# Who makes the low parts of w1's and w2's words: from GpSimd and three VectorE passes to VectorE and, for half of them, a second ScalarE pass

## The chip, the core and the metric

The kernel runs on one core of a Trainium2 chip (trn2). A core has five engines that run side by side, each taking its own instructions strictly in the order in which the program put them: TensorE (PE in the profile; the load of its weights is PEld), VectorE (DVE), ScalarE (ACT), GpSimd (POOL) and SyncE (SP, which here only issues DMAs). SBUF is the on-chip memory of 128 partitions, PSUM the accumulator that TensorE writes. The metric is the device time of one execution in microseconds (us); lower is better.

## The reference

Three layers stand one behind the other. Causal attention with a decay bias over 4 batches, 8 heads, 576 positions and a head size of 64; then a gated product through four weights; then a soft mixture of 8 experts. What matters here is the second layer:

```python
def _moe_ref(x, w1, w2, w3, w_out):      # x 2304x512, w1 and w2 512x1024
    a = x @ w1
    b = x @ w2
    h = a * b @ w3
    return (h @ w_out).astype(np.float32)
```

The four weights reach the chip as 64-bit floats, seen as pairs of 32-bit words, and the kernel makes 32-bit floats of them itself.

## The kernel before

The attention comes first, per item (a head and some of its five query tiles): `att_scores` multiplies on PE into a PSUM tile `sc_ps` (L359), takes bias, mask and row maximum on DVE (L362) and the exponent on ACT (L367). `att_norm` sums and inverts on DVE (L376, L377) and scales the tile `sc` by the inverse on POOL (L380). `att_transpose` turns `sc` on PE (`pt_ps` L395, `ptd_ps` L409) and copies it on ACT (L397, L411), and `att_pv` multiplies by the values on PE (`x_ps`, L110) and splits the result into a high and a low part on ACT and DVE (L444, L445).

The gated product `glu_half` (L457, `gl`) multiplies a split x by a split weight: high by high, low by high and high by low, for four blocks of 128 rows, so twelve matmuls for one PSUM tile. Its weights are the tiles `w12t_0` to `w12t_7`, each with a high and a low part, and each made of two halves of 128x512 words. So w1 and w2 are 16 halves, k = 0 to 15, and `load_words(k)` handles one of them:

- SP fetches 512 KB into `raw_w` (L188; three such buffers, NRAW = 3, so the fetch of half k + 3 waits until half k's words have been read).
- `convert` makes the float `w`. With `by_act` false: one ACT pass scales the upper word (L202), and three DVE passes shift (L205), put in the sign (L206) and put in the lower word's bits (L209). With `by_act` true: a second ACT pass turns the lower word in place (L213), and two DVE passes join the three (L214, L217). Before the change w1 and w2 take the first form; the 24 halves of `wot` and `w3t` that follow take the second.
- ACT rounds `w` to the high part (L233), and POOL subtracts to get the low part (L234).

The order in which the Python code calls these steps is woven from lists (`weave`): the halves 0 to 7 among the attention's first part, 8 to 15 further on among the first gated products. The order on PE, DVE, ACT and POOL is then set by a scheduler that reckons its own times, so an edit in one place reorders the queues around it and behind it; SP's order is the written one. The scores use four PSUM tiles in turn, the values and the transposes two each.

Of the kernel before, what the change touches and what calls it, by code (L numbers as in the profile page):

```python
# [10 lines left out]
F32 = mybir.dt.float32  # L11
# [5 lines left out]
ALU = mybir.AluOpType  # L17
# [30 lines left out]
def attn_glu_softmoe_kernel(  # L48
# [14 lines left out]
    nc = tc.nc  # L63
# [127 lines left out]
    def convert(k, w, by_act, behind=None):  # L191
        raw = words.pop(k)
        pair = raw.bitcast(I32).rearrange("p (n t) -> p n t", t=2)
        hi, lo = pair[:, :, 1], pair[:, :, 0]
        wi, wu = w.bitcast(I32), w.bitcast(U32)
        order = mybir.DependencyInfo(mybir.DependencyClass.NoSync, mybir.DependencyReason.DATA)

        def line_up(step):
            if behind is not None:
                tc.add_manual_dep(step.ins, behind.ins.name, order, reason="order")  # L200

        line_up(nc.scalar.activation(out=w, in_=hi.bitcast(F32), func=AF.Copy, scale=F64_SCALE))  # L202
        lu = lo.bitcast(U32)
        if not by_act:
            nc.vector.tensor_scalar(out=wi, in0=wi, scalar1=3, scalar2=None, op0=ALU.logical_shift_left)  # L205
            nc.vector.scalar_tensor_tensor(  # L206
                out=wi, in0=hi, scalar=-0x80000000, in1=wi, op0=ALU.bitwise_and, op1=ALU.bitwise_or
            )
            return nc.vector.scalar_tensor_tensor(  # L209
                out=wu, in0=lu, scalar=29, in1=wu, op0=ALU.logical_shift_right, op1=ALU.bitwise_or  # L210
            )

        line_up(nc.scalar.activation(out=lo, in_=lu, func=AF.Copy, scale=LO_SCALE, bias=-0.49999))  # L213
        nc.vector.scalar_tensor_tensor(  # L214
            out=wi, in0=wi, scalar=3, in1=lo, op0=ALU.logical_shift_left, op1=ALU.bitwise_or
        )
        return nc.vector.scalar_tensor_tensor(  # L217
            out=wi, in0=hi, scalar=-0x80000000, in1=wi, op0=ALU.bitwise_and, op1=ALU.bitwise_or
        )
# [4 lines left out]
    def load_words(k, ap):  # L224
        (kind, i), e = TODO[k // 2], k % 2
        span = slice(512 * e, 512 * e + 512)
        if kind == "w12":
            if e == 0:
                w12_t[i] = wp.tile([P, 2, 2, KC, P], F32R, tag="W", name=f"w12t_{i}", bufs=NW)
            w = gq.tile([P, 512], F32, tag="g4", name=f"w_{kind}_{i}_{e}", bufs=NG4)  # L230
            convert(k, w, False)
            th, tl = (w12_t[i][:, n].rearrange("p a k f -> p (a k f)")[:, span] for n in range(2))
            nc.scalar.copy(out=th, in_=w)  # L233
            nc.gpsimd.tensor_tensor(out=tl, in0=w, in1=th.bitcast(F32), op=ALU.subtract)  # L234
        elif k < 2 * N0:
            if e == 0:
                rows_t[kind, i] = gq.tile([P, FC, P], F32, tag="g4", name=f"{kind}_{i}", bufs=NG4)
            rows_w[kind, i] = convert(k, rows_t[kind, i].rearrange("p c f -> p (c f)")[:, span], True)
        else:
            if e == 0:  # L240
                rows_t[kind, i] = ap.tile([P, 1024], F32, tag="words", name=f"w_{kind}_{i}", bufs=NRAW)
            convert(k, rows_t[kind, i][:, span], True, st["a_copy"])
# [514 lines left out]
    with tc.tile_pool(name="att", bufs=1) as ap:  # L757
# [11 lines left out]
            out=mask[:, S - P :], in_=mask[:, S - P :], pattern=[[-1, P]], base=0,  # L769
# [27 lines left out]
        def load(k):  # L797
            i = k // 2 - 1
            if FC <= i < N0:
                (sum_rows if k % 2 else use_rows)(*TODO[i])  # L800
            if k < 2 * N0:
                load_words(k, ap)
            if k + NRAW < 2 * N0:
                fetch_words(k + NRAW, ap)
# [10 lines left out]
        for i in range(N0, len(TODO)):  # L815
            more += [(1, lambda i=i: fetch_later(i)), (1, lambda: None)]
            more += [(1, lambda k=2 * i + e: load_words(k, ap)) for e in range(2)] + [(1, lambda: None)]
# [8 lines left out]
        k = GC - GB  # L826
# [75 lines left out]
    for a in range(0, 4, 2):  # L902
        zt_ps = psum("tp", f"zt_ps_{a}")
        for c in range(2):
            nc.tensor.transpose(zt_ps[:, c * P : (c + 1) * P], z_acc[:, (a + c) * P : (a + c + 1) * P], ident)
        nc.vector.tensor_reduce(
            out=zt[:, a : a + 2], in_=zt_ps[:, : 2 * P].rearrange("p (c t s) -> p c s t", t=2, s=2 * NS),
# [233 lines left out]
```

## Time and profile before

| what | value |
| --- | --- |
| median of 3 runs | 550.09 us (549.1 to 554.26) |
| the profiled execution | 552.43 us, of which the span from first to last instruction is 550.7 us |
| PE busy | 516.8 us, 94% of the span |
| DVE busy | 329.0 us, 60% |
| ACT busy | 311.6 us, 57% |
| POOL busy | 130.6 us, 24% |

A busy PE is not yet a PE at its peak, since the ends of its matmuls are modelled. Shares of busy time are means over stages that have different limits, so the rows further down are taken by stage: to 46 us the attention stands nearly alone, from 46 to 83 us attention, the words of w1 and w2 and the first gated products run together, to 175 us the words of `wot` and `w3t` join, and from there to 490 us gated products, attention and the experts' gates fill PE.

### The profile page before, as it was taken

To read this page: it belongs to the slowest core of one execution; us is meant where nothing else is said; L and a number is where in the kernel's file an instruction comes from. 1 tells how busy PE (TensorE), PEld (TensorE's weight loads), DVE (VectorE), ACT (ScalarE), POOL (GpSimd) and SP (SyncE) were. 2 spreads that over 40 slices of the span, in tenths; PEclk is the share of its full clock that TensorE was granted. 3 is DMA by queue.
4 is the path that set the end of the run, shared out by engine and by line. 5 is a ranking of instruction groups with operands and counts; after the bars stand their busy time and mean duration, and the time that the engine had idled before them with its cause. 6 is when DMAs were issued, how large, how long until landed. Compare 5 with 4: busy or idle time off the path is not lost.

```text
span 550.7 us, 11764 instructions
## 1 busy us (share of the span) xinstructions
PE 516.8 (94%) x4288; PEld 434.3 (79%) x4288; DVE 329.0 (60%) x1016; ACT 311.6 (57%) x845; POOL 130.6 (24%) x199
## 2 busy tenths in 40 slices
PE   2799899998999999999999999999999999989993
PEld 2567678877788898999989889899989999843452
DVE  7558787879987394866577668566630311252433
ACT  4567667687986674866577567558644211321222
POOL 4475563102454232110221311111310000000000
PEclk9999989999999999999999999999999999999998
DMA  5746973977673253563656537553514999689977
GB/s 147 235 146 193 280 223 128 292 259 269 218 253 102 73 161 113 169 201 133 194 170 211 173 99 208 176 172 114 167 44 137 413 411 376 241 293 423 420 295 241
DMA packets 38809, 118.03 MB, mean 214 GB/s; under 512 B 4224, under 2 KB 10560, under 8 KB 35296
## 3 DMA queue, kind: packets, MB, share of 16 engines
q1 hardware_dynamic: 36768, 113.60, 61.0%
q10 hardware_dynamic: 1984, 3.69, 2.4%
q8 instruction: 34, 0.56, 0.4%
q14 instruction: 23, 0.19, 0.1%
HBM read 102.11 MB, written 11.60 MB: 206 GB/s over the span
## 4 chain that ended last, share of the span: by engine, by line
PE 70%; DMA 13%; DVE 8%; ACT 4%; issue 2%; POOL 1%; SPq 0%; ACTq 0%; DVEq 0%; POOLq 0%
PE gl L457 31%; PE sc_ps L359 7%; PE x_ps L110 7%; PE pt_ps L395 5%; DMA raw_w<-in_w 5%; PE gn_ps L627 3%; PE o_ps L1042 3%; DMA raw_w3t<-in_w3t 3%; PE h_ps L1004 3%; PE ptd_ps L409 2%; PE z_ps L110 2%; DMA raw_wot<-in_wot 2%; DVE sc L362 1%; PE lg L110 1%; ACT sc L367 1%
## 5 line engine op out<-in xcount | busy, mean ns | idle before, releaser
L457 PE MATMUL gl<-x,w12t 128*128 128x320 f32 (+1 forms) x1536 | 237.7, 304 | 0.1
L457 PEld LDWEIGHTS gl<-x,w12t 128*128 128x128 f32 x1536 | 212.7, 190 | 7.4 <-issue 4.4
L380 POOL TENSOR_SCALAR sc<-sc,rinv 128x64 f32<-128x64 f32 (+4 forms) x160 | 101.1, 650 | 253.0 <-DVE rinv L377 85.7
L367 ACT ACTIVATE sc<-sc,nmax 128x64 f32<-128x64 f32 (+4 forms) x160 | 89.8, 563 | 31.4 <-DVE nmax L362 29.1
L362 DVE CUSTOM_DVE_ANT_0 sc<-sc_ps,mask 128x64 f32<-128x64 f32 (+4 forms) x160 | 65.0, 423 | 31.8 <-PE sc_ps L359 31.0
L397 ACT COPY pt<-pt_ps 128x128 f32<-128x128 f32 (+3 forms) x128 | 53.0, 426 | 34.1 <-PE pt_ps L395 25.1
L395 PE MATMUL pt_ps<-ident,sc 128*128 128x128 f32 x320 | 56.6, 286 | 5.5 <-POOL sc L380 3.2
L395 PEld LDWEIGHTS pt_ps<-ident,sc 128*128 128x128 f32 x320 | 38.4, 144 | 16.9 <-POOL sc L380 7.2
L463 ACT COPY a<-gl 128x256 f32<-128x256 f32 (+1 forms) x64 | 25.4, 398 | 46.0 <-PE gl L457 40.7
L359 PE MATMUL sc_ps<-qa 128*128 128x64 f32 (+1 forms) x144 | 46.4, 334 | 1.3 <-DVE gT L475 0.8
L110 PE MATMUL x_ps<-pt,v 128*64 128x256 f32 (+1 forms) x384 | 47.4, 358 | 0.0
L359 PE MATMUL sc_ps<-raw 68*128 68x288 f32 (+4 forms) x96 | 35.8, 516 | 11.6 <-DMA raw<-rows 9.8
L359 PE MATMUL sc_ps<-qb 68*128 68x64 f32 (+1 forms) x144 | 43.6, 306 | 0.9 <-DMA qb<-qa 0.9
L110 PEld LDWEIGHTS x_ps<-pt,v 128*64 128x64 f32 x384 | 33.5, 140 | 5.8 <-issue 1.0
L359 PEld LDWEIGHTS sc_ps<-raw 68*128 68x128 f32 x96 | 21.6, 265 | 16.9 <-issue 14.1
L202 ACT ACTIVATE w_w<-raw_w 128x512 f32<-128x512 f32 x32 | 21.6, 676 | 17.8 <-DMA raw_w<-in_w 17.7
L445 DVE TENSOR_TENSOR x<-x_ps,x 128x320 fp32r<-128x320 f32 (+1 forms) x32 | 14.1, 452 | 29.2 <-ACT x L444 29.2
L630 ACT COPY gn<-gn_ps 128x512 f32<-128x512 f32 x40 | 22.5, 584 | 15.5 <-PE gn_ps L627 15.1
L367 ACT ACTIVATION_READ_ACCUMULATOR sc<-sc,nmax 128x1 f32 x160 | 30.9, 193 | 0.0
L359 PEld LDWEIGHTS sc_ps<-qa 128*128 128x128 f32 x144 | 27.4, 190 | 3.6 <-DVE gT L475 1.3
L409 PE MATMUL ptd_ps<-ident,sc 128*128 128x128 f32 x160 | 25.9, 286 | 3.2 <-ACT pt L397 3.0
L359 PEld LDWEIGHTS sc_ps<-qb 68*128 68x128 f32 x144 | 27.4, 191 | 1.6 <-DVE v_sb L276 1.0
(180 smaller groups left out, 725.6 us busy)
## 6 DMA issues: line engine op xcount, KB each, us to landing
ew<-in_ew SPq DMA_DIRECT2D x27, 1024.0 KB
raw_w<-in_w SPq DMA_DIRECT2D x32, 512.0 KB
raw<-in_qk SPq DMA_DIRECT2D x24, 576.0 KB
v<-in_v SPq DMA_DIRECT2D x16, 576.0 KB
raw_w3t<-in_w3t SPq DMA_DIRECT2D x16, 512.0 KB
raw_wot<-in_wot SPq DMA_DIRECT2D x8, 512.0 KB
raw_wo<-in_wo SPq DMA_DIRECT2D x8, 512.0 KB
w_d<-w_w SPq DMA_DIRECT2D x8, 512.0 KB
```

What stands on the lines that cost most here:

```text
L110: mm = nc.tensor.matmul(out_, lhs, rhs, start=start, stop=stop)
L202: line_up(nc.scalar.activation(out=w, in_=hi.bitcast(F32), func=AF.Copy, scale=F64_SCALE))
L359: nc.tensor.matmul(pp[:r, : z - a], x[:, 0, q0 : q0 + r], x[:, 1, a:z], start=x is mul[0], stop=x is mul[-1])
L362: nc.vector.tensor_tensor_reduce(out=sc[:r, a:z], in0=pp[:r, : z - a], in1=hd["mask"][:r, m0 : m0 + z - a], scale=-0.125, scalar=3.0e38 if ...
L367: nc.scalar.activation(out=sc[:r, :W], in_=sc[:r, :W], func=AF.Exp, bias=nmax[:r, i : i + 1], scale=-1.0, accum_out=rsum[:r, i, 0:1],)
L380: nc.gpsimd.tensor_scalar(out=sc, in0=sc, scalar1=rinv[:, i : i + 1], scalar2=1.0, op0=ALU.mult, op1=ALU.mult)
L395: nc.tensor.transpose(tp[:, j * P : (j + 1) * P], sc[:, j * P : (j + 1) * P], ident)
L397: t["turned", i] = nc.scalar.copy(out=pt[:, p0 : p0 + step * (i - 1) + 1 : step], in_=tp[:, : i * P].rearrange("p (j q) -> p j q", q=P))
L409: nc.tensor.transpose(dg[:, p0 : p0 + P], t["sc"][:, c0 : c0 + P], ident)
L457: nc.tensor.matmul(acc[:, :nt], w12_t[fc][:, wi, n, kc], x_t[b, blk, kc][:, xi], start=k == 0, stop=k == 3 * KC - 1)
L463: st["a_copy"] = nc.scalar.copy(out=a_sb[:, :nt], in_=acc[:, :nt])
L630: st["turned", blk, k, h] = nc.scalar.copy(out=gn[:r, 4 * h : 4 * h + 4].rearrange("p c f -> p (c f)"), in_=tp[:r])
```

## The change

Two things change in `load_words`. The low part's subtraction goes from POOL to DVE, for all 16 halves. And `convert` is called with `k >= 8` in the place of `False`, so the last eight halves are converted in the second form: two ACT passes and two DVE passes in the place of one and three.

```diff
@@ load_words
             w = gq.tile([P, 512], F32, tag="g4", name=f"w_{kind}_{i}_{e}", bufs=NG4)
-            convert(k, w, False)
+            convert(k, w, k >= 8)
             th, tl = (w12_t[i][:, n].rearrange("p a k f -> p (a k f)")[:, span] for n in range(2))
             nc.scalar.copy(out=th, in_=w)
-            nc.gpsimd.tensor_tensor(out=tl, in0=w, in1=th.bitcast(F32), op=ALU.subtract)
+            nc.vector.tensor_tensor(out=tl, in0=w, in1=th.bitcast(F32), op=ALU.subtract)
```

SP's queue is the same before and after. On the other engines instructions move. The next rows are POOL's, from the stretch around 46 to 83 us (`w_w_4_0` is half 8: tile 4, half 0; `rinv` comes from L377):

```order
 L380 TENSOR_SCALAR sc_632<-sc_632,rinv_725 128x576
-L234 TENSOR_TENSOR w12t_664<-w_w_4_0_665,w12t_664 128x512
-L234 TENSOR_TENSOR w12t_664<-w_w_4_1_716,w12t_664 128x512
-L234 TENSOR_TENSOR w12t_761<-w_w_5_0_762,w12t_761 128x512
 L380 TENSOR_SCALAR sc_696<-sc_696,rinv_807 128x448
 L380 TENSOR_SCALAR sc_696<-sc_696,rinv_807 128x576
-L234 TENSOR_TENSOR w12t_761<-w_w_5_1_819,w12t_761 128x512
-L234 TENSOR_TENSOR w12t_879<-w_w_6_0_880,w12t_879 128x512
-L234 TENSOR_TENSOR w12t_879<-w_w_6_1_932,w12t_879 128x512
 L380 TENSOR_SCALAR sc_802<-sc_802,rinv_895 128x448
 L380 TENSOR_SCALAR sc_802<-sc_802,rinv_895 128x576
```

Only the attention's scalings stay on POOL, in their old order. On PE, at about 77 us of the trace of before, this piece changes (`sc_802` is the tile that POOL's last two rows above scale):

```order
 L359 MATMUL sc_ps_4_1_903<-raw_585 128x288
-L409 MATMUL ptd_ps_860<-ident,sc_696 128x128 x2
-L395 MATMUL pt_ps_3_912<-ident,sc_802 128x128 x3
 L457 MATMUL gl_0_2_1_917<-x_0_0_111,w12t_433 128x320 x3
 L457 MATMUL gl_0_2_1_917<-x_0_1_157,w12t_433 128x320 x3
 L457 MATMUL gl_0_2_1_917<-x_0_2_181,w12t_433 128x320 x3
 L457 MATMUL gl_0_2_1_917<-x_0_3_253,w12t_433 128x320 x3
+L409 MATMUL ptd_ps_860<-ident,sc_696 128x128 x2
+L395 MATMUL pt_ps_3_912<-ident,sc_802 128x128 x3
```

The transposes of `sc_802` now stand behind twelve gated products, which stood behind them. On DVE, where half 8 and half 9 are converted, before:

```order
L205 TENSOR_SCALAR w_w_4_1_716<-w_w_4_1_716 128x512
L206 SCALAR_TENSOR_TENSOR w_w_4_1_716<-raw_w_4_1_560,w_w_4_1_716 128x512
L209 SCALAR_TENSOR_TENSOR w_w_4_1_716<-raw_w_4_1_560,w_w_4_1_716 128x512
L362 ISA sc_696,nmax_695<-sc_ps_3_0_697,mask 128x448
```

and the same place on DVE now:

```order
L214 SCALAR_TENSOR_TENSOR w_w_4_1_716<-w_w_4_1_716,raw_w_4_1_560 128x512
L234 TENSOR_TENSOR w12t_664<-w_w_4_0_665,w12t_664 128x512
L217 SCALAR_TENSOR_TENSOR w_w_4_1_716<-raw_w_4_1_560,w_w_4_1_716 128x512
L362 ISA sc_696,nmax_695<-sc_ps_3_0_697,mask 128x448
L362 ISA nmax_695 128x1
L362 ISA sc_696,nmax_695<-sc_ps_4_0_730,mask 128x288
L362 ISA nmax_695 128x1
L234 TENSOR_TENSOR w12t_664<-w_w_4_1_716,w12t_664 128x512
```

Each subtraction stands a few instructions behind the last pass on its words: that of half 8 between the two passes on half 9, that of half 9 between two pieces of the attention's maximum (L362). It reads what ACT's L233 wrote, so DVE now waits there for ACT, as POOL did.

## Rows read from the trace of the kernel before

**Rows 1.** Windows by stage: PE, PEld, DVE, ACT, POOL busy (count), PEclk, DMA, GB/s
```profile
7.00:46.00 39.00, 31.97 (x120) 24.10 (x121) 23.76 (x94) 24.16 (x79) 19.27 (x30) 1.00 0.58 168
46.00:83.00 37.00, 33.02 (x216) 26.41 (x215) 31.43 (x72) 25.85 (x64) 22.58 (x18) 0.95 0.83 244
...
175.00:490.00 315.00, 313.59 (x2645) 284.91 (x2643) 170.14 (x553) 176.01 (x487) 51.08 (x92) 1.00 0.57 192
```
**Rows 2.** Waits of PE, 46 to 83 us: total, times, longest
```profile
PE pt_ps L395 <- ACT pt L397: 1.9, 2, 0.9
PE pt_ps L395 <- POOL sc L380: 1.2, 1, 1.2
PE sc_ps L359 <- DVE w_w L205: 0.6, 1, 0.6
```
**Rows 3.** Timeline of PE: start, us, line, tile, [idle before <- releaser]
```profile
78.66 0.68 PE L395 MATMUL pt_ps<-ident,sc 128*128 128x128 f32 x3 [1.19 <-POOL sc L380]
78.99 3.52 PE L457 MATMUL gl<-x,w12t 128*128 128x320 f32 x12
...
86.28 2.14 PE L457 MATMUL gl<-x,w12t 128*128 128x320 f32 x12
```
**Rows 4.** Timeline of POOL around 77 us
```profile
75.83 1.46 POOL L234 TENSOR_TENSOR w12t<-w_w,w12t 128x512 fp32r<-128x512 f32 x1 [1.28 <-ACT w12t L233]
77.27 2.48 POOL L380 TENSOR_SCALAR sc<-sc,rinv 128x448 f32<-128x448 f32 x2
```
**Rows 5.** Windows of 1 us: granted clock of PE is the third number from the end
```profile
78.00:79.00 1.00, 0.34 (x4) 0.35 (x4) 1.00 (x3) 0.82 (x2) 1.00 (x2) 0.97 0.35 115
79.00:80.00 1.00, 1.00 (x6) 1.00 (x5) 0.97 (x2) 0.00 (x0) 1.00 (x2) 0.50 0.90 254
82.00:83.00 1.00, 1.00 (x6) 0.73 (x4) 0.15 (x1) 1.00 (x4) 0.68 (x1) 0.83 0.83 250
```
**Rows 6.** Groups of POOL, ACT and DVE, 46 to 83 us: busy, mean ns, idle before
```profile
L234 POOL TENSOR_TENSOR w12t<-w_w,w12t 128x512 fp32r<-128x512 f32 x10 | 14.7, 1480 | 12.8 <-ACT w12t L233 12.8
L380 POOL TENSOR_SCALAR sc<-sc,rinv 128x448 f32<-128x448 f32 (+1 forms) x8 | 8.0, 1009 | 2.8 <-DVE rinv L377 2.6
...
L233 ACT CAST w12t<-w_w 128x512 fp32r<-128x512 f32 x10 | 6.2, 623 | 3.4 <-DVE w_w L209 3.4
L397 ACT COPY pt<-pt_ps 128x384 f32<-128x384 f32 (+3 forms) x13 | 5.5, 428 | 1.5 <-PE pt_ps L395 1.5
L202 ACT ACTIVATE w_w<-raw_w 128x512 f32<-128x512 f32 x8 | 5.4, 679 | 5.5 <-DMA raw_w<-in_w 5.4
...
L209 DVE SCALAR_TENSOR_TENSOR w_w<-raw_w,w_w 128x512 uint32<-128x512 uint32 x10 | 12.5, 1252 | 0.2
L206 DVE SCALAR_TENSOR_TENSOR w_w<-raw_w,w_w 128x512 int32<-128x512 int32 x9 | 6.9, 768 | 0.1
L205 DVE TENSOR_SCALAR w_w<-w_w 128x512 int32<-128x512 int32 x9 | 3.8, 422 | 3.5 <-ACT w_w L202 3.4
```
**Rows 7.** Single lines, whole span: count, ns min/median/max, first and last start
```profile
L209 DVE SCALAR_TENSOR_TENSOR w_w<-raw_w,w_w x16: 673/1043/1646, 9.3 to 79.2; 128x512 uint32<-128x512 uint32 x16
L214 DVE SCALAR_TENSOR_TENSOR w_w<-w_w,raw_w x16: 682/693/1093, 285.3 to 408.3; 128x512 int32<-128x512 int32 x16
L217 DVE SCALAR_TENSOR_TENSOR w_w<-raw_w,w_w x16: 678/682/823, 287.1 to 409.2; 128x512 int32<-128x512 int32 x16
L213 ACT ACTIVATE raw_w<-raw_w x16: 660/668/717, 284.6 to 407.6; 128x512 int32<-128x512 uint32 x16
```
**Rows 8.** Timeline of DVE and of POOL at 48 us
```profile
48.57 1.65 DVE L209 SCALAR_TENSOR_TENSOR w_w<-raw_w,w_w 128x512 uint32<-128x512 uint32 x1
...
48.00 1.66 POOL L234 TENSOR_TENSOR w12t<-w_w,w12t 128x512 fp32r<-128x512 f32 x1 [3.46 <-ACT w12t L233]
```
**Rows 9.** PE's transposes (L395), to 46 us and from 46 to 77 us: ns min/median/max
```profile
L395 PE MATMUL pt_ps<-ident,sc x15: 421/421/476, 15.3 to 44.2; 128*128 128x128 f32 x15
...
L395 PE MATMUL pt_ps<-ident,sc x30: 271/273/329, 46.6 to 73.4; 128*128 128x128 f32 x30
```
## The prediction

> **What bounds the kernel now.** I read the windows by stage first. From 175 to 490 us PE is busy for 313.59 of 315 us [rows 1]: whatever comes early, PE works it off without a gap, so time won or lost ahead of 175 us arrives at the end nearly whole. The edit's own instructions all lie ahead of 83 us (L209 starts for the last time at 79.2 us [rows 7]). So the question is what PE loses there. Between 46 and 83 us it is busy for 33.02 of 37 us, DVE for 31.43, ACT for 25.85, POOL for 22.58 [rows 1]: PE lacks 3.98 us, DVE is next to full.
>
> Second, I read PE's waits in that window. The long ones are 1.9 us for ACT's copies of transposed tiles, 1.2 us for POOL's scaling (L380) and 0.6 us for DVE [rows 2]. The place of the 1.2 us is at 78.66 us: PE waits 1.19 us for `sc_802` [rows 3]. POOL began that scaling at 77.27 us, the moment at which it finished a subtraction (L234) that had started at 75.83 us [rows 4]. So here the instruction that the edit takes away stands right in front of the one that PE needs.
>
> Third, the granted clock. The gap is followed by a fall: 0.97 in the microsecond in which PE was busy for only 0.34, then 0.50 from 79 us, and 0.83 in the microsecond from 82 [rows 5]. 0.50 is the 1.2 GHz level, 1.00 the 2.4 GHz one. The twelve gated products at 78.99 us took 3.52 us, the same twelve at 86.28 us took 2.14 us [rows 3].
>
> **The change part by part.**
>
> *The wait on POOL.* Without L234, POOL is free when L377 gives the inverse, at most 1.2 us earlier for PE; and the order of after puts twelve gated products (2.14 us at full clock) ahead of the transposes of `sc_802`, more than the gap. I take all of it: -1.2 us. Bounds 0 (another releaser steps in) and -1.2.
>
> *The clock.* If that gap goes, the half-speed stretch goes: full cycles lost are 0.03 + 3 x 0.50 + 0.17 = 1.7 us by the windows 78 to 83 (I show the first, one of three and the last) [rows 5]. The gated products alone give 3.52 - 2.14 = 1.4. I take -1.7; bounds 0 and -1.7.
>
> *DVE, last eight halves.* In 46 to 83 us ten L209, nine L206 and nine L205 took 12.5 + 6.9 + 3.8 = 23.2 us [rows 6]. In their place stand two halves in the old form with a subtraction, and eight in the new one. The subtraction on DVE at this size is in no row. Nearest is L214, two inputs from SBUF at 128x512, 0.693 us; L209's 0.673 and 1.646 are the ends for two inputs at this size [rows 7]. I take 0.69. A new half is 0.693 + 0.682 + 0.69 = 2.07 us; an old one 0.42 + 0.69 + 0.69 + 0.69 = 2.49 without slowing. Together 8 x 2.07 + 2 x 2.49 = 21.5, less 1.1 for the L205 and L206 that fall ahead of 46 us: 20.4. DVE gets back 2.8 us, if the slowing goes away. At 1.646 a piece the ten subtractions cost 9.6 us more, and DVE loses 6.8.
>
> *Why the slowing should go.* L209 takes 0.673 us at its fastest and 1.25 in the mean of this stage [rows 6, 7]. At 48.57 us it took 1.65 us beside a POOL subtraction of 48.00 to 49.66 us, which was itself slowed to 1.66 us; 49.66 + 0.56 is L209's end at 50.22 [rows 8], so one ran behind the other. With the subtraction on DVE that partner is gone. The scalings remain, 8.0 us of POOL in the window [rows 6].
>
> What DVE's 2.8 us are worth to PE: PE waited for DVE directly for only 0.6 us here [rows 2], so between 0 and -1.5 us (that 0.6 and 0.9 of ACT's copies behind it). I take -0.5.
>
> *DVE, first eight halves.* Their passes stay, and each gets a subtraction. Six of the eight lie ahead of 46 us (ten of L209's sixteen lie behind it [rows 6, 7]): 6 x 0.69 = +4.1 us on a DVE that is busy for 23.76 of 39 us [rows 1]. PE, busy for 31.97, is the slower one there, so DVE's 15.2 idle us hide it: 0. Without that cover, up to +4.1.
>
> *ACT.* Eight more passes of 0.668 us [rows 7] make 5.3 us. ACT is idle for 11.15 us from 46 to 83 us, of which 5.4 us it waits for words to land and 3.4 us for L209 [rows 1, 6]. A pass fits into these idles as a sum, but it stands in front of copies that PE waits for: queued behind L202 and L213 are L397 and L411, and PE already waits for L397 for 1.9 us [rows 2]. I take one pass in front of one such copy: +0.6 us. Bounds 0 and +1.9 (both waits grow by one pass and a half).
>
> *DMA.* SP's queue is unchanged. A `raw_w` buffer is freed by L217 in the place of L209, the same number of steps behind its landing (L202, L213, L214, L217 for L202, L205, L206, L209), so refetches start when they did: 0.
>
> Sum: -1.2 - 1.7 - 0.5 + 0.6 = -2.8 us against the profiled execution's 552.43 us, so 549.6. That run lies 0.4% above the median of 550.09; scaled, 547.3 us.
>
> **The rivals.**
>
> *The clock rises earlier (faster).* The same transposes take 421 ns up to 44.2 us and 273 ns from 46.6 us [rows 9]. So PE runs slowly through the first stage, although the granted clock reads 1.00 there, and I go by durations. PE is busy for 31.97 of 39 us in it [rows 1]. If the new order on PE lets the clock rise a quarter of the stage earlier, some 34 us in the place of 44, ten busy microseconds shrink to 10 x 273 / 421 = 6.5: -3.5 us. With the sum's -2.8 and DVE's full -1.5 in the place of -0.5 that is -7.3, so 543. Against it: transfers of the next heads' rows pace that stage too.
>
> *DVE takes over POOL's wait (slower).* POOL sat idle for 12.8 us from 46 to 83 us until ACT's L233 came [rows 6], and that cost only POOL. Now DVE waits there, with L362 behind it, which frees the scores' PSUM for PE. If each of the eight late subtractions holds DVE for two of ACT's copies that stand ahead of L233 and for L233, 2 x 0.428 + 0.623 = 1.48 us [rows 6], that is 11.8 us; less the 2.8 us saved and DVE's 5.6 us of idle time [rows 1], 3.4 us reach PE, and a gap of this kind brings one more fall of the clock beside the old one: 3.4 + 1.2 + 1.7 = +6.3, so 556.5 us. It decides from (2.8 + 5.6) / 8 = 1.05 us a half. Against it: each subtraction stands behind passes on the next half, by which time L233 is mostly done, and DVE already waited 3.4 us for ACT there.
>
> *The scalings take the subtraction's place (no change).* A half of the new form has three passes with two SBUF inputs, the old one has two. Rows 8 show such a pass and a POOL instruction one behind the other. If each of the eight scalings in the window, 8.0 us in all [rows 6], holds DVE for its whole length, DVE loses 8.0 - 2.8 = 5.2 us, all but 0.4 of its idle time. L377 then comes late by about the time that POOL is free sooner, PE waits at the same place for the same scaling, and the clock falls as before: 0, so 550. Against it: the scalings fill 8.0 of 37 us, so most passes meet none. The Trainium skill's page "SBUF — State Buffer", section "Who interferes with whom", states what this rival rests on: a VectorE instruction with two SBUF inputs and a GpSimd instruction that reads SBUF exclude each other for the whole instruction. By that rule, rows 8 agree, and the edit trades one partner of the exclusion for more meetings with the other.
>
> **How the numbers follow.** The forecast, 547.3 us with its own range of 545 to 549.5 us, has 0.45; the early clock 0.30 (543, within 538 to 544.5); DVE's wait 0.15 (556.5, from 555.7 on); the scalings 0.10. One per cent, 5.5 us, is about what a measurement of this kernel can tell from no change. So faster by more than 1% has 0.30, within 1% 0.55, slower 0.15. The range, 540 to 554 us, leaves out the slower case and the far end of the early clock, some 0.2.
>
> **What would show it.** Right: no granted clock below 1.00 between 46 and 83 us, no PE wait for L380 over 0.5 us there, L214 and L217 near 0.69 us, PE idle in that window near 1.5 us less than 3.98. DVE's rival shows as idle time ahead of L234 put down to L233 beyond 1 us a half and as PE waits for L362. The early clock shows in transposes of 273 ns well before 44 us. Wrong it would be if the windows after 175 us were no longer full, or if a gap over 1 us with a fall of the clock came back elsewhere ahead of 100 us.

## The result and the profile after

The changed kernel takes 556.84 us (median of 12 runs, 553.19 to 561.16) against 551.38 us before (12 runs, 548.22 to 554.26) on the same chip: ratio 1.0101, interval 1.0077 to 1.0126. It is slower by 1%, where 547.3 us was forecast and 554 was the upper end. The profiled execution of after is its fastest one (553.19 us, span 551.4 us), that of before lies above its median, so their spans differ by only 0.7 us, and no row of the two profiles can stand for the difference of the medians.

The windows by stage, in the columns of [rows 1], from the trace of after:

```profile
7.00:46.00 39.00, 32.06 (x107) 22.36 (x109) 27.26 (x103) 24.06 (x78) 12.82 (x24) 1.00 0.58 162
46.00:83.00 37.00, 34.03 (x219) 26.24 (x216) 24.90 (x62) 27.58 (x67) 7.75 (x9) 0.91 0.74 217
...
175.00:490.00 315.00, 313.08 (x2652) 284.24 (x2648) 170.25 (x554) 177.42 (x492) 54.07 (x95) 1.00 0.57 191
```

What the edit was to do, it did. From 46 to 83 us DVE is busy for 24.90 us in the place of 31.43, POOL for 7.75 in the place of 22.58, and PE lacks 2.97 us in the place of 3.98. The groups of the same window, beside [rows 6], show how (busy, mean ns, idle before):

```profile
L380 POOL TENSOR_SCALAR sc<-sc,rinv 128x448 f32<-128x448 f32 (+2 forms) x9 | 8.2, 924 | 27.3 <-DVE rinv L377 16.1 <-ACT raw_w L213 8.4 <-ACT x L444 2.7
...
L217 DVE SCALAR_TENSOR_TENSOR w_w<-raw_w,w_w 128x512 int32<-128x512 int32 x8 | 5.8, 724 | 0.0
...
L214 DVE SCALAR_TENSOR_TENSOR w_w<-w_w,raw_w 128x512 int32<-128x512 int32 x8 | 5.5, 692 | 4.7 <-ACT raw_w L213 4.7
L234 DVE TENSOR_TENSOR w12t<-w_w,w12t 128x512 fp32r<-128x512 f32 x8 | 5.5, 686 | 0.4 <-ACT w12t L233 0.2
...
L213 ACT ACTIVATE raw_w<-raw_w 128x512 int32<-128x512 uint32 x8 | 5.3, 668 | 0.0
L233 ACT CAST w12t<-w_w 128x512 fp32r<-128x512 f32 x8 | 5.0, 629 | 1.4 <-DVE w_w L209 1.4
```

The subtraction costs 0.686 us on DVE, 0.69 had been taken; L209, 1.25 us in the mean of [rows 6], is at 0.69 again (one instruction in this window; all eight of after took 676 to 727 ns). The wait of 1.2 us for POOL [rows 2, 3] is gone, and the clock no longer falls behind it [rows 5]. PE's two long waits in the window are new (total, times, longest):

```profile
PE ptd_ps L409 <- ACT pt L397: 1.6, 1, 1.6
PE gl L457 <- ACT x L444: 1.0, 1, 1.0
```

The mean granted clock of the window is 0.91, lower than the 0.95 before. The windows of 1 us say where; the granted clock is the third number from the end:

```profile
47.00:48.00 1.00, 0.70 (x4) 0.29 (x2) 1.00 (x4) 0.27 (x1) 0.03 (x1) 1.00 0.00 0
48.00:49.00 1.00, 0.00 (x0) 0.00 (x0) 0.75 (x3) 1.00 (x3) 0.00 (x0) 1.00 0.70 184
...
51.00:52.00 1.00, 1.00 (x4) 0.59 (x3) 0.00 (x0) 0.57 (x2) 0.14 (x1) 0.62 0.95 361
52.00:53.00 1.00, 1.00 (x3) 0.49 (x2) 0.39 (x1) 0.00 (x0) 0.00 (x0) 0.50 0.91 240
...
57.00:58.00 1.00, 1.00 (x13) 0.81 (x10) 0.00 (x0) 0.00 (x0) 0.90 (x2) 0.50 0.00 0
58.00:59.00 1.00, 1.00 (x13) 0.75 (x11) 0.17 (x1) 0.90 (x4) 0.46 (x1) 0.97 0.00 0
```

PE is idle for most of 47.7 to 49.3 us, the clock falls at 51 us, and PE works at the 1.2 GHz level until 58 us. Full cycles lost: 0.38 + 6 x 0.50 + 0.03 = 3.4 us, twice what the fall at 79 us had cost. The durations show something more, which the granted clock doesn't: in after the transposes of L395 still take 421 to 476 ns at 47.0 to 47.3 us, and those of L409 take 272 to 334 ns from 49.3 us; in before both take 270 to 274 ns from 46.3 us. So PE also reaches the 2.4 GHz level for the first time some 3 us later, and in after it holds it only until 51 us. PE's timeline there, first of before, then of after (start, us, line, tile, [idle before <- releaser]):

```profile
44.37 2.10 PE L359 MATMUL sc_ps<-raw 68*128 68x448 f32 x6
...
47.52 1.96 PE L359 MATMUL sc_ps<-raw 68*128 68x448 f32 x6 [0.61 <-DVE w_w L205]
...
49.78 1.12 PE L457 MATMUL gl<-x,w12t 128*128 128x320 f32 x6
```

```profile
40.99 3.75 PE L359 MATMUL sc_ps<-raw 68*128 68x448 f32 x6
...
49.32 0.55 PE L409 MATMUL ptd_ps<-ident,sc 128*128 128x128 f32 x3 [1.63 <-ACT pt L397]
...
51.05 3.44 PE L359 MATMUL sc_ps<-raw 68*128 68x448 f32 x6
53.88 2.21 PE L457 MATMUL gl<-x,w12t 128*128 128x320 f32 x6
```

These are the same instructions (the profile counts each of the score instructions twice, so x6 stands for three): the scores of item 8 (2.10 before, 3.75 after), the scores of item 9 (1.96, 3.44), the first six gated products (1.12, 2.21), and the gap ahead of them (0.61, 1.63). Together after loses 1.65 + 1.48 + 1.09 + 1.02 = 5.2 us on four rows. That the medians differ by 5.5 us proves nothing by itself, since the two profiled spans differ by 0.7 us: this execution of before paid its 1.2 and 1.7 us at 78 us, and after didn't. The rows show where to look. What differs is the order: after makes the scores of item 8 ahead of the transposes of item 4 and of the values product of items 2 and 3, before made them behind that product, between item 4's transposes. The experiments ask whether it is this order, and which part of the edit brought it.

### The profile page after: what moved, and what is told of

Same layout as the page of the kernel before. It is cut to its first block, busy times and chain, and to the rows that moved or that the text cites. A ratio compares the mean times of both kernels' runs of the same rounds, so it can differ in the third digit from the quotient of the medians.

```text
span 551.4 us, 11754 instructions
## 1 busy us (share of the span) xinstructions
PE 518.7 (94%) x4288; PEld 433.5 (79%) x4288; DVE 328.4 (60%) x1024; ACT 316.3 (57%) x853; POOL 112.5 (20%) x183
## 4 chain that ended last, share of the span: by engine, by line
PE 69%; DMA 12%; DVE 7%; ACT 6%; issue 2%; POOL 1%; SPq 1%; ACTq 0%; DVEq 0%; POOLq 0%
PE gl L457 31%; PE x_ps L110 7%; PE sc_ps L359 6%; DMA raw_w<-in_w 6%; PE pt_ps L395 5%; PE gn_ps L627 3%; PE o_ps L1042 3%; DMA raw_wot<-in_wot 3%; PE h_ps L1004 3%; PE ptd_ps L409 2%; PE z_ps L110 2%; DMA raw_w3t<-in_w3t 2%; DVE sc L362 1%; POOL sc L380 1%; PE lg L110 1%
## 5 line engine op out<-in xcount | busy, mean ns | idle before, releaser
L380 POOL TENSOR_SCALAR sc<-sc,rinv 128x64 f32<-128x64 f32 (+4 forms) x160 | 105.3, 677 | 291.0 <-DVE rinv L377 175.3
L362 DVE CUSTOM_DVE_ANT_0 sc<-sc_ps,mask 128x64 f32<-128x64 f32 (+4 forms) x160 | 65.1, 423 | 35.3 <-PE sc_ps L359 32.3
L395 PE MATMUL pt_ps<-ident,sc 128*128 128x128 f32 x320 | 56.0, 287 | 4.5 <-POOL sc L380 3.2
L395 PEld LDWEIGHTS pt_ps<-ident,sc 128*128 128x128 f32 x320 | 37.9, 145 | 16.2 <-issue 8.0
L359 PE MATMUL sc_ps<-raw 68*128 68x288 f32 (+4 forms) x96 | 39.6, 556 | 11.6 <-DMA raw<-rows 9.8
L359 PE MATMUL sc_ps<-qa 128*128 128x64 f32 (+1 forms) x144 | 45.8, 331 | 1.9 <-DVE nmax L362 1.0
L110 PE MATMUL x_ps<-pt,v 128*64 128x256 f32 (+1 forms) x384 | 46.4, 361 | 0.0
L110 PEld LDWEIGHTS x_ps<-pt,v 128*64 128x64 f32 x384 | 32.1, 142 | 7.0 <-issue 2.0
L409 PE MATMUL ptd_ps<-ident,sc 128*128 128x128 f32 x160 | 26.5, 291 | 2.7 <-ACT pt L397 2.6
L214 DVE SCALAR_TENSOR_TENSOR w_w<-w_w,raw_w 128x512 int32<-128x512 int32 x24 | 17.2, 716 | 18.4 <-ACT raw_w L213 18.3
```

The costliest lines, as they stand in the source:

```text
L110: mm = nc.tensor.matmul(out_, lhs, rhs, start=start, stop=stop)
L359: nc.tensor.matmul(pp[:r, : z - a], x[:, 0, q0 : q0 + r], x[:, 1, a:z], start=x is mul[0], stop=x is mul[-1])
L362: nc.vector.tensor_tensor_reduce(out=sc[:r, a:z], in0=pp[:r, : z - a], in1=hd["mask"][:r, m0 : m0 + z - a], scale=-0.125, scalar=3.0e38 if ...
L380: nc.gpsimd.tensor_scalar(out=sc, in0=sc, scalar1=rinv[:, i : i + 1], scalar2=1.0, op0=ALU.mult, op1=ALU.mult)
L395: nc.tensor.transpose(tp[:, j * P : (j + 1) * P], sc[:, j * P : (j + 1) * P], ident)
L409: nc.tensor.transpose(dg[:, p0 : p0 + P], t["sc"][:, c0 : c0 + P], ident)
```

## The experiments

Each ratio is to runs of before on the same chip. In the table, the columns behind the ratio come from the timelines of each kernel's one profiled execution: when the first six gated products start and how long they take (1.12 us at the 2.4 GHz level, 2.21 at 1.2 GHz), and when SP issues the fetch of the values v_7.

| kernel | ratio, 95% interval | gl starts, us | six gl, us | v_7, us |
| --- | --- | --- | --- | --- |
| before | 1 | 49.8 | 1.12 | 44.0 |
| after | 1.0101, 1.0077 to 1.0126 | 53.9 | 2.21 | 47.1 |
| e1 subtraction only | 1.0077, 1.0051 to 1.0103 | 52.4 | 2.21 | 46.6 |
| e2 ACT pass only | 1.0090, 1.0058 to 1.0122 | 46.6 | 1.12 | 40.7 |
| e3 after again | 1.0102, 1.0051 to 1.0154 | 54.1 | 2.22 | 47.9 |
| e5 after's work, before's order | 1.0071, 1.0038 to 1.0104 | 49.0 | 1.12 | 43.5 |
| e6 before's work, after's order | 1.0087, 1.0054 to 1.0120 | 52.9 | 2.21 | 46.2 |
| e7 one subtraction, half 6 | 1.0005, 0.9980 to 1.0031 | 48.5 | 1.95 | 40.7 |
| e8 one subtraction, half 12 | 0.9987, 0.9959 to 1.0015 | 49.2 | 1.12 | 43.7 |
| e9 after, place 1 on ACT | 1.0121, 1.0094 to 1.0148 | 53.1 | 2.21 | 45.6 |
| e10 after, places 1 and 2 on ACT | 1.0135, 1.0115 to 1.0155 | 55.1 | 2.21 | 47.5 |
| e11 before, one cast moved | 1.0018, 0.9998 to 1.0037 | 49.1 | 1.12 | 43.1 |
| e12 as e5, ACT passes paired | 1.0027, 1.0006 to 1.0048 | 47.8 | 1.12 | 42.1 |
| e13 before's head, after's tail | 0.9998, 0.9969 to 1.0026 | 48.9 | 1.12 | 43.1 |
| e14 after's head, before's tail | 1.0147, 1.0112 to 1.0182 | 55.0 | 2.21 | 47.6 |
| e15 after, three scores moved | 1.0129, 1.0091 to 1.0167 | 57.4 | 1.95 | 48.2 |
| e16 before, six scores moved | 1.0111, 1.0076 to 1.0147 | 52.4 | 2.21 | 45.8 |
| e17 after, values later | 1.0063, 1.0023 to 1.0102 | 53.3 | 2.22 | 46.5 |
| e18 before, values later | 0.9948, 0.9919 to 0.9977 | 45.6 | 1.12 | 41.0 |

### Each part of the edit alone (e1 to e4)

```diff
-            nc.gpsimd.tensor_tensor(out=tl, ...)          e1: this line alone
+            nc.vector.tensor_tensor(out=tl, ...)
-            convert(k, w, False)                          e2: this line alone
+            convert(k, w, k >= 8)
```

> Only the subtraction (L234) goes to VectorE, all 16 halves stay in the old form. Up to 46 us every queue stands as in the changed kernel. Theory A (the loss comes from the order of the first 50 us, which the subtraction on VectorE sets: ScalarE casts and exponents stand in front of the copies that TensorE waits for near 47 us, and TensorE's clock then stays at its lower level for some 7 to 10 us more): 1.007 to 1.013 of before, 555 to 558 us, and a wait of TensorE for L397 over 1 us near 47 us with transposes at 421 ns beyond 48 us. Theory B (the loss comes from the second ScalarE pass of the last eight halves): 0.995 to 1.003, 549 to 553 us.

> Only the last eight halves take the second form, the subtraction stays on GpSimd. Up to 46 us every queue stands as in the kernel before. Theory A (order of the first 50 us): 0.995 to 1.004 of before, 549 to 553 us, clock up near 44 us as before, no gap near 47 us. Theory B (second ScalarE pass): 1.007 to 1.013, 555 to 558 us, with more waits of TensorE for ScalarE copies between 50 and 85 us.

> The changed kernel once more, for a second profile. Its first profile was 553.2 us where its median is 556.8, so a usual run should show more lost than that profile does. Theory A: TensorE's transposes at 421 ns until 55 us or later, or a stretch of granted clock 0.50 longer than the 7 us of the first profile, in the first 100 us. Rival C (the usual loss lies behind 100 us, in the stage of the words of wot and w3t): the first 100 us as in the first profile, and falls of the clock or gaps of TensorE between 100 and 175 us worth 3 us more.

> The kernel before once more, for a second profile. 549 to 554 us. Theory A: transposes at 421 ns until about 44 us as in its first profile, and at most one short fall of the clock before 100 us. If its clock rises 5 us or more later and the time is still that of before, theory A loses its price.

Each part alone costs 0.8 to 0.9%, both together 1.0%: they don't add up, as two prices of passes would. Up to 46 us e1 has after's queues and e2 has before's, and the table shows that e1 has the slow first products and e2 has not. A second profile of before (e4, 553.03 us) loses 3.4 us of full cycles in other falls, from 68 to 76 us: single executions differ by several us in where the clock falls, so single profiles can't be subtracted from each other to a microsecond. A second profile of after (e3, 559.0 us) has the fall at 51 us again, 3.4 us of full cycles, and more behind it: 1.7 us from 71 us and 3.4 us between 150 and 175 us. So part of what a long execution of after loses lies behind 100 us.

### Work and order apart (e5 to e8, e12)

The scheduler set a new order for all engines: on PE 1502 of 3440 instructions kept their place. But for the moved passes both kernels make the same instructions in the same sequence of code, so an order can be carried over, with order-only dependences that make nothing wait on another engine:

```python
ins = list(tc.nc.cur_bb.bb.instructions)
for chain in ORDER:                       # PE, ACT, DVE, POOL: the other kernel's order
    for a, b in zip(chain, chain[1:]):
        tc.add_manual_dep(ins[b], ins[a].name, NO_SYNC, reason="order")
```

e5 is after with before's order, e6 is before with after's. e7 and e8 are before with a single subtraction on DVE, as a change of order with next to no change of work:

```diff
-            nc.gpsimd.tensor_tensor(out=tl, ...)
+            (nc.vector if k == 6 else nc.gpsimd).tensor_tensor(out=tl, ...)
```

> This kernel does all of after's work, but every PE, ACT, DVE and POOL instruction that both kernels have on the same engine stands in before's order; only the sixteen subtractions and the eight second ACT passes find their own places between them. Theory O (the loss comes from the new order that the scheduler derives for all engines, not from the work that was moved): about before's time, ratio 0.99 to 1.003. Theory W (the moved passes themselves cost it, on DVE and ACT): about after's time, ratio 1.007 to 1.013.

> The converse: before's work (subtractions on POOL, one ACT pass for every half), with every PE, ACT, DVE and POOL instruction that both have in after's order. Theory O: about after's time, ratio 1.007 to 1.013, with the first gated products near 53 us in the place of 49.8. Theory W: about before's time, ratio 0.997 to 1.003, with the first gated products back near 50 us.

> Before with one change: the subtraction of half 6 alone goes to DVE, 0.69 us of work once. The scheduler reorders more than half of PE's rows behind it. Theory O in its strong form (before's order is a good one among many, and nearly any other loses): ratio 1.004 to 1.012 although next to no work has moved. Theory O in its weak form (only the orders that after's larger edits bring are bad) and theory W: ratio 0.997 to 1.003.

> As the run before, for the subtraction of half 12 alone; PE's rows change only behind the first 226, in the stretch from some 50 us on. Theory O, strong: ratio 1.004 to 1.012. Theory O, weak, and theory W: 0.997 to 1.003. If this one is flat and the run before is not, the loss needs a new order ahead of 50 us.

e6 is as slow as after without one moved pass: the order alone costs 0.9%. e7 and e8 are flat, so not any new order loses (in e7 PE ran at the upper level from about 35 us and fell back later). But e5 lost too, 0.7%. Its trace shows one place, PE first, then ACT:

```profile
60.30 0.52 PE L395 MATMUL pt_ps<-ident,sc 128*128 128x128 f32 x3 [3.59 <-ACT pt L397]
```

```profile
58.72 0.67 ACT L213 ACTIVATE raw_w<-raw_w 128x512 int32<-128x512 uint32 x1 [2.86 <-DMA raw_w<-in_w]
59.28 0.61 ACT L233 CAST w12t<-w_w 128x512 fp32r<-128x512 f32 x1
59.78 0.37 ACT L397 COPY pt<-pt_ps 128x256 f32<-128x256 f32 x1
```

The second ACT passes had been left to find their places, and one stood ahead of a copy for PE and waited 2.86 us for its words; PE waited 3.59 us behind it. That is the wait which the prediction priced at 0.6, at another place. e12 puts each second pass directly behind its first:

```diff
 ACT's chain of e5, for each of the last eight halves
-  ..., L202 (half k), ..., L213 (half k) wherever the scheduler likes
+  ..., L202 (half k), L213 (half k), ...
```

> The run of after's work in before's order once more, with each second ACT pass (L213) fixed directly behind the first pass (L202) of its half; in that run the scheduler had put it ahead of L202 and ahead of copies, where it waited 2.86 us for words, with PE's gap of 3.59 us at 60.30 us behind it. Theory S: that gap is below 1.2 us here, and the ratio to before falls from 1.007 to 0.996 to 1.002. Theory W (the moved passes cost it wherever they stand): 1.005 to 1.010.

The loss falls to 0.3%, between the bounds given for the two theories. So all the moved work, in an order that suits it, costs 0.3 to 2.6 us, and its place in ACT's queue can cost as much again.

### Two places on ACT (e9 to e11)

In after ACT stands waiting with copies behind it. The timeline ahead of PE's gap at 49.32 us:

```profile
47.73 0.62 ACT L233 CAST w12t<-w_w 128x512 fp32r<-128x512 f32 x1 [1.36 <-DVE w_w L209]
48.26 0.77 ACT L367 ACTIVATE sc<-sc,nmax 128x576 f32<-128x576 f32 x1
...
49.03 0.24 ACT L397 COPY pt<-pt_ps 128x128 f32<-128x128 f32 x1
```

e9 moves the copies ahead of the casts, e10 does the same at the second wait, at 69 us; e11 moves one cast in before to where after has it:

```diff
 ACT's chain, e9 (from after)                  ACT's chain, e11 (from before)
-  L233 L367 L233 L367 L397 L444 L397 L411     -  L397 L444 L397 ... L411 L397 L233
+  L397 L233 L367 L444 L397 L233 L411 L367     +  L397 L444 L233 L397 ... L411 L397
```

> After in its own order on every engine, but for one place on ACT: the first copy of pt_428 (L397) moved ahead of both casts (L233) of w12t_552, and the copies behind it (L444, L397, L411) moved ahead of the second cast or of the exponent behind it. Theory S (the loss lies at the places where passes on words stand ahead of copies on ACT, as gap of PE and as the fall of the clock behind it): PE's gap of 1.63 us at 49.32 us below 0.5 us, no granted clock under 0.9 between 50 and 60 us, and so up to 1.6 + 3.4 = 5 us less: ratio to before 1.000 to 1.005. Rival N (a gap at 50 us is absorbed behind it, since words and rows arrive no earlier): 1.008 to 1.012, as after.

> As the run before, and a second place on ACT: the copies L444 of x_253 and L397 of pt_678 moved ahead of the two passes (L202, L213) of the half that follows. Theory S: the gap of 1.0 to 2.3 us that PE has at 69 to 71 us ahead of gl (for ACT's x, L444) goes too, ratio to before 0.997 to 1.003. Rival N: 1.008 to 1.012.

> Before in its own order on every engine, but for one place on ACT: the cast L233 of the first half of w12t_552, which waits for DVE's L209 until 46.8 us, is moved ahead of the copy L397 of pt_428's second part, as in after. Not a pass more or less. Theory S: PE gets a gap of 1.5 to 2.5 us between 45 and 49 us and the granted clock falls behind it by 1.7 to 3.4 us: ratio 1.004 to 1.010. Rival N: the gap is there and the time is not, ratio 0.998 to 1.003.

This theory fell. In e9 the one gap became three, and the clock fell as in after; PE's timeline:

```profile
47.35 0.30 PE L395 MATMUL pt_ps<-ident,sc 128*128 128x128 f32 x1 [0.77 <-ACT pt L397]
48.68 0.41 PE L395 MATMUL pt_ps<-ident,sc 128*128 128x128 f32 x2 [1.02 <-ACT ptd L411]
49.51 0.79 PE L409 MATMUL ptd_ps<-ident,sc 128*128 128x128 f32 x3 [0.42 <-ACT pt L397]
50.09 3.62 PE L359 MATMUL sc_ps<-raw 68*128 68x448 f32 x6
```

Two heads' transposes follow each other with nothing between them; there are two PSUM tiles for them, so each third set waits for an ACT copy, whatever ACT does first. In before the scores of items 8 and 9 lie between them. And e11, with a gap of 1.04 us at 46.58 us behind its moved cast, kept the clock; its 0.2% is not clear of the noise (0.9998 to 1.0037). e11 also has before's order fixed by the same dependences, so fixing an order costs 0.4% at most.

### Head, tail, and six products on PE (e13 to e16)

At the transposes of item 8's upper tiles (58.6 us in before, 62.9 us in after) both orders have the same set of instructions behind them on PE, ACT, DVE and POOL. There head and tail can be joined crosswise, all with after's work: e13 has before's head (as e12) and after's tail, e14 the converse.

```diff
 every engine's chain
-  after's order
+  e13: before's order for the first 129 PE, 81 ACT, 113 DVE, 44 POOL instructions, then after's
+  e14: after's order for the same ones, then before's
```

> After's work on every engine in before's order (second ACT passes directly behind the first) up to the transposes of sc_563, 58.6 us in the profile of before, and in after's order from there. Up to this place both orders have the same set of instructions on PE, ACT, DVE and POOL, so only their sequence differs. Theory H (after's order loses ahead of this place): ratio to before 1.000 to 1.005, and the clock does not fall between 50 and 58 us. Theory L (it loses behind it): 1.007 to 1.013.

> The converse: after's work, in after's order up to the transposes of sc_563 and in before's order from there. Theory H: ratio to before 1.007 to 1.013, with the clock at 0.50 between 51 and 58 us as in after. Theory L: 1.000 to 1.005.

The loss is in the head: 0.9998 with before's head, 1.0147 with after's. These two differ in the tail as well, so the head's price comes from the pairs that share a tail: with after's tail 1.0% (after, 1.0101, against e13, 0.9998), with before's tail 1.2% (e14, 1.0147, against e12, 1.0027). Only the sequence of the same instructions up to that place differs in each pair; this is the cleanest comparison of the study. By the medians after's tail is 0.3 to 0.5% better than before's, with intervals that overlap. In the two profiles the place itself comes at 57.5 us in e13 and at 64.5 us in e14.

In e14 there is no fall of the granted clock behind PE's gap; by the durations PE hadn't reached the upper level yet (its L395 takes 415 ns and more from 57.0 to 59.7 us). So the first products can be slow without a fall ahead of them. Its timeline and window:

```profile
55.00 2.21 PE L457 MATMUL gl<-x,w12t 128*128 128x320 f32 x6
```

```profile
55.00:56.00 1.00, 1.00 (x5) 0.86 (x4) 0.51 (x3) 1.00 (x4) 0.00 (x0) 1.00 0.22 82
```

e15 and e16 move nothing but scores on PE:

```diff
 e16, PE's chain of before (x_ps_2 = values product of items 2 and 3)
+  sc_ps_8_3 sc_ps_8_4 sc_ps_8_4
   pt_ps_4 x_ps_2 ... pt_ps_4
-  sc_ps_8_3 sc_ps_8_4 sc_ps_8_4
   ptd_ps_4 pt_ps_5
-  sc_ps_9_3 sc_ps_9_4 sc_ps_9_4
   pt_ps_5 ptd_ps_5
+  sc_ps_9_3 sc_ps_9_4 sc_ps_9_4
 e15, PE's chain of after
+  sc_ps_9_3 sc_ps_9_4 sc_ps_9_4
   ptd_ps_4 pt_ps_5 ptd_ps_5
-  sc_ps_9_3 sc_ps_9_4 sc_ps_9_4
```

> After in its own order, but for three instructions on PE: the scores sc_ps_9_3_0, 9_4_0 and 9_4_1 (L359, 2.1 us at the lower clock) stand ahead of the transposes ptd_ps of pair 4 in the place of behind those of pair 5, so that two heads' transposes no longer follow each other bare at 47 to 51 us. Theory P (the bunched transposes, each waiting for an ACT copy, leave PE idle and the clock then falls to 0.50 for 7 us): PE's idle time between 47 and 51 us, 2.5 us in after, falls below 1.2 us, the fall of the clock behind it goes or is at most half as long, ratio to before 1.002 to 1.006. Rival N (the fall near 51 us comes whatever stands there): 1.008 to 1.013.

> Before in its own order, but for six instructions on PE: the scores of item 8 stand ahead of the first transpose of pair 4, and those of item 9 behind the last transpose of pair 5, as in after, so that the transposes of two heads follow each other bare. Theory P: PE gets 1 to 2 us of idle time between 44 and 50 us and the clock falls behind it for some us; ratio 1.003 to 1.008. Rival N: 0.998 to 1.003.

e16 has before's passes, before's queues on ACT, DVE and POOL, and six PE instructions in other places: it is as slow as after, 1.0111. Its timeline of PE and two of its windows of 1 us:

```profile
40.95 2.65 PE L359 MATMUL sc_ps<-raw 68*128 68x448 f32 x6 [1.68 <-DVE rinv L377]
...
48.52 0.41 PE L395 MATMUL pt_ps<-ident,sc 128*128 128x128 f32 x2 [1.51 <-ACT ptd L411]
...
49.26 3.75 PE L359 MATMUL sc_ps<-raw 68*128 68x448 f32 x6
52.39 2.21 PE L457 MATMUL gl<-x,w12t 128*128 128x320 f32 x6
```

```profile
47.00:48.00 1.00, 0.01 (x1) 0.00 (x0) 1.00 (x4) 0.73 (x3) 0.00 (x0) 1.00 0.79 268
...
49.00:50.00 1.00, 1.00 (x4) 0.56 (x3) 0.97 (x4) 0.96 (x4) 0.86 (x1) 0.50 1.04 323
```

The gap of 1.51 us and the low level until 56 us are like those of after. But the move did more: item 8's scores waited 1.68 us at 40.95 us, which after doesn't have, a first fall of the clock followed from 42 to 46 us (1.7 us of full cycles), and the fetch of v_7 went out 1.8 us later. So e16 shows what the place of six instructions costs, and not that the bare transposes alone cost it. e15 shows that putting back one half of it in after doesn't help, for a reason that is not on PE:

```profile
51.47 3.75 PE L359 MATMUL sc_ps<-raw 68*128 68x448 f32 x6 [2.71 <-DMA raw<-rows_d]
```

The scores of item 9 were moved ahead, but their rows came at 51.4 us. The reason stands in SP's queue, here of before, then of after:

```profile
43.99 0.33 SPq L308 DMA_DIRECT2D v<-in_v  x1
44.38 0.32 SPq L324 DMA_DIRECT2D raw<-rows_d  x1
...
45.97 0.52 SPq L188 DMA_DIRECT2D raw_w<-in_w  x1
```

```profile
47.12 0.33 SPq L308 DMA_DIRECT2D v<-in_v  x1
47.50 0.32 SPq L324 DMA_DIRECT2D raw<-rows_d  x1
...
49.10 0.52 SPq L188 DMA_DIRECT2D raw_w<-in_w  x1
```

The fetch of v_7 waits until the values product of items 2 and 3 has read its buffer. SP's wait there, put down to PE's L110, is 4.7 us in before and 8.1 us in after. After makes item 8's scores first, so this product ends 3.1 us later, and behind the fetch the rows of item 9 and the words of half 8 are late by as much. SP's order is the same in both kernels; its times are not.

### The fetch of the values one item later (e17, e18)

```diff
-            prep = [(0, lambda n=n: att_values(n + 1, ap))] if n + 1 < N else []
+            prep = [(0, lambda n=n: att_values({4: 0, 5: 5, 6: 0, 7: 7}.get(n, n + 1), ap))] if n + 1 < N else []
```

> After in its own order on PE, ACT, DVE and POOL, but on SP the fetches of v_5 and v_7 (L308), which wait for a buffer until the values product of an earlier pair is done, stand one item later, behind the rows and the words that stood behind them. Theory V (in after PE makes that product 3 us later, since it makes the scores of item 8 first; the rows and words queued on SP behind the fetch are late by as much, and this stage is paced by its transfers): the fetch of half 8's words is issued below 44 us in the place of 49.1 us, DMA share from 40 to 60 us at least 0.6 in the place of 0.46, and the ratio to before falls from 1.010 to 0.995 to 1.004. Rival P (the order on PE itself costs it, by gaps and clock): 1.008 to 1.013.

> The same two fetches one item later in before, all other engines in before's own order. Theory V: SP's waits of 8 and 4.4 us for these two buffers go, words and rows come earlier, ratio 0.990 to 0.999. Rival P: 0.998 to 1.003, since nothing changes on PE.

The windows (DMA share and GB/s are the last two numbers) show the transfers moved ahead, of after and then of e17:

```profile
26.00:40.00 14.00, 13.42 (x55) 9.98 (x54) 11.40 (x48) 10.79 (x39) 7.87 (x14) 1.00 0.58 163
40.00:60.00 20.00, 17.97 (x84) 11.85 (x84) 11.08 (x32) 12.00 (x32) 5.84 (x9) 0.83 0.46 129
```

```profile
26.00:40.00 14.00, 12.91 (x52) 9.44 (x51) 10.82 (x47) 10.43 (x36) 7.72 (x14) 1.00 0.88 231
40.00:60.00 20.00, 18.98 (x94) 13.29 (x92) 12.39 (x34) 12.39 (x34) 5.72 (x9) 1.00 0.34 107
```

In e17 the words of half 8 are issued at 37.68 us in the place of 49.10, yet the ratio is still 1.0063, and the first six products take 2.22 us. The ratio lies between the bounds of the two theories. So the late fetches are a part at most (the interval, 1.0023 to 1.0102, overlaps that of after, so even a part is not shown), and the order on PE with its level of the clock remains. In before the same edit is worth 0.5%: e18 takes 548.87 us against 550.34, ratio 0.9948 (0.9919 to 0.9977), and is faster than both kernels.

## Why the prediction was wrong

**The step that failed is "DVE, first eight halves: 0", and with it the way in which the sum was made.** Six subtractions were added to a DVE with 15.2 us of idle time, and their own time was hidden but for little: PE waited once for a subtraction, 1.4 us at 19.69 us, where before waited 0.95 us for rows, and e13 has such a wait of 1.0 us and no loss. But the scheduler set a new order around them ahead of 46 us, and this order was priced nowhere. The four joins of head and tail show that the head's sequence alone is worth 1.0 to 1.2%, e16 that the place of six score products on PE suffices for 1.1%, e6 that no moved pass is needed. The prediction had the new order of PE at hand and read it at one place only, at 78 us, where it spoke for the change.

**The wait on POOL (-1.2) and the clock (-1.7)** came true in the trace: no gap for L380 and no granted clock below 1.00 from 78 to 83 us. But as a gain they were oversized, since before doesn't always pay them. Its own second profile (e4) has no wait for L380 there and runs twelve gated products at 77.64 us in 2.00 us; its clock fell elsewhere, from 68 us, behind a wait of 1.33 us for ACT. e11 has before's order on PE; its timeline and windows at the same place:

```profile
77.32 0.55 PE L395 MATMUL pt_ps<-ident,sc 128*128 128x128 f32 x3 [0.97 <-POOL sc L380]
77.62 2.00 PE L457 MATMUL gl<-x,w12t 128*128 128x320 f32 x12
```

```profile
77.00:78.00 1.00, 0.68 (x5) 0.68 (x6) 0.96 (x3) 0.48 (x2) 1.00 (x2) 1.00 0.51 139
78.00:79.00 1.00, 1.00 (x9) 1.00 (x8) 1.00 (x2) 0.01 (x1) 1.00 (x2) 1.00 0.93 373
```

A gap of 0.97 us for the same scaling, and no fall. The profiled run of before stood 0.4% above its median; the prediction scaled that away, where it should have asked which event in the trace made this run slower than the others. The fall that it meant to win back was one such event, as far as these two other profiles show.

**DVE, last eight halves (-0.5 at PE).** The prices were right: L214, L217 and the subtraction took 692, 724 and 686 ns, and the slowing of L209 went. DVE's busy time in the window fell by 6.5 us, not by 2.8, for another reason: the window of after holds eight subtractions and one half of the old form where ten and two had been reckoned (18.2 us of passes in the place of 20.4), and 1.5 us less of other instructions. The rule of the Trainium skill's page "SBUF — State Buffer", section "Who interferes with whom", on which the third rival rested, is that a VectorE instruction with two SBUF inputs and a GpSimd instruction that reads SBUF exclude each other. The trace agrees, with [rows 8] and with L209's return to 0.69 us, but the partner that stayed, the scalings, cost little (means of 692 and 724 ns against medians of 693 and 682 in [rows 7]). No gain of PE shows from it.

**ACT (+0.6, bounds 0 and +1.9).** All moved passes together cost 0.06 to 0.48% in e12, 0.3 to 2.6 us, so the size was fair for passes in a good order. In e5 one of them in a bad place cost 2.86 us of ACT, beyond the upper bound.

**DMA: 0.** Wrong. SP's order is unchanged, and the buffers of the words were looked at, but not the values' buffers that stand in the same queue: v_7 goes out at 47.12 us in the place of 43.99, with rows and words behind it.

**The rivals.** The clock was named as the lever of this stage, with the wrong sign: the rival let it rise earlier and win, and in truth it rose later than before and, but for 49.3 to 51 us, PE stayed at the lower level until 58 us. DVE waited for L233 for 0.2 us, not for 1.05 us a half, so this slower rival came to the right side of the result by a mechanism that isn't there: luck. Its sum also adds 1.2 us to the 3.4 us of gap without a reason. That the stretch from 175 us on stays full held (313.08 of 315 us), so what is lost ahead of it arrives at the end. The range lacked the case that happened: the scores of items 8 and 9 and the first gated products at the lower level, with a gap near 48 us, out of the new order. The text named it only as what would make the forecast wrong.

**What stays open.** e2 (the second ACT pass alone, in the scheduler's own order) has a fast head and still loses 0.9%; its trace shows gaps of 1.27 us at 140.70 and 1.64 us at 167.29 us, both behind ACT copies, but this wasn't tested. That the clock's level carries the head's loss is read from the durations of the same instructions; no run changed the clock alone, or the gap without the fetches. e15's move together with e17's was not tried.

## What to carry to other kernels

Where a scheduler derives the order, an edit's price is the price of the new order: compare the order on the bounding engine from the first difference on, not only at the wait that the edit should remove, and look for runs of small dependent instructions from which the long ones have been moved away. Carry one kernel's order over to the other's work, and join head and tail crosswise: that tells work from order and finds the place, if all four combinations are run and those with the same tail are compared. And before crediting the removal of a stall, ask whether a second profile has it too, above all when the profiled run is slower than the median.

## What the runs showed of the hardware

- A gap of about 1 us on PE was followed by a fall of the clock in one execution and by none in another: 1.19 us at 78.66 us with a fall to 0.50 [rows 3, 5], 0.97 us at 77.32 us and 1.04 us at 46.58 us in e11 with none.
- The granted clock reads 1.00 in stretches in which the durations show the lower level. In e14 the first six gated products took 2.21 us with the granted clock at 1.00 in every window from 44 to 60 us; in after they took 2.21 us at 0.50, in before 1.12 us at 1.00. Ahead of the first rise the durations alone tell the level.
- A DMA queue whose order is unchanged still moved by 3.1 us, since one fetch in it waits for a buffer that PE frees.
